# The last block's x in weight buffers, attention placed by time, and the ring's space given up a block sooner

## Chip, core and metric

One NeuronCore of one Trainium2 chip runs the kernel. TensorE (PE) does the matrix products, VectorE (DVE), ScalarE (ACT) and GpSimd (POOL) the elementwise work, and SyncE (SP) issues nearly all DMAs, in the order in which they stand in its queue. The metric is the device time of one execution in microseconds (us), as the median of several runs.

## What is computed

```python
# attention, float32, q, k, v: 4 x 8 heads x 768 x 64; chunks of 32 queries
for c in range(nc):
    k_ctx = k[:, :, l_start:r_end]           # 16 keys left, 8 right of the chunk
    k_full = np.concatenate([mem_k, k_ctx], axis=2)   # v_full likewise
    scores = scale * np.matmul(q_c, k_full.transpose(0, 1, 3, 2))
    scores = scores - np.max(scores, axis=-1, keepdims=True)
    a = np.exp(scores)
    a = a / (np.sum(a, axis=-1, keepdims=True) + 1e-09)
    out[:, :, c_start:c_end] = np.matmul(a, v_full)
# x: 3072 tokens x 512; two layers in a row, 512 -> 2048 -> 512
h = x @ w_in;  g = h - np.tanh(h);  x = g @ w_out
h = x @ w_in2; g = np.maximum(h, 0) + alpha * np.minimum(h, 0); out = g @ w_out2
```

## The kernel before

Every float32 operand of a product is split into a high and a low part (`hi`, `lo`), and three products stand for one (hi·hi, hi·lo, lo·hi).

**Attention** goes by 24 tiles of 128 tokens (t = 0 to 23). For one tile: scores on PE (`sp`, L654), maximum and subtraction on DVE (`mx`, L678; `sc`, L680), exponential on ACT (L722), sum and reciprocal on DVE (`sg`, L733 to L735), the scaling on POOL (`sc`, L740), a transpose on DVE (`et`, L748), copies into `ebuf` on ACT (L761) and POOL (L759), and the values on PE (`pv`, L779). ACT (L788) and DVE (L791) then write the tile's x, in a high and a low part, into the **ring**: two tiles with 8 slots of 128 tokens, in SBUF space of its own.

**Layer 1** goes by 6 blocks of 4 tiles (b = 0 to 5; `blocks1`, N1 = 6). Within a block a loop runs over 16 slices f of the hidden dimension: `h` (L300) is 12 products over x from the ring, then g is made (tanh on ACT, subtraction on DVE, `gh` on ACT L321, `gl` on POOL L322), then `y` (L355) is 12 products. In blocks 4 and 5 only `h` runs, and g is kept (`ga`, `gb`, L336 and L337): their second product is made with layer 2's scheme, one level of a seven-product algorithm, whose products `yb` (L552) follow block 5. Each f has two positions, so that a block is 32 positions; position 0 is the first of block 0.

**Where attention stands.** Blocks use ring slots 0 to 3 and 4 to 7 in turn. `release` in the planning code says from which position a tile may be written: when the block that used its slots has ended. Tiles 20 to 23 (block 5) use the slots of block 3 and may start only at position 127, the end of block 3. The plan keeps steps at least `SPACE` = 6 positions apart, whatever a position lasts (in blocks 4 and 5 it lasts half as long), and step t holds the values of tile t-1 and the scores of tile t. By these rules steps 18 to 24 stand at positions 101, 107, 113, 127, 133, 142 and 148. Loads of a tile's k and q stand LP = 3 positions ahead of its step, the softmax 2 behind it.

**Parking.** Layer 2's weights arrive as float64 (`pk`, L100). They are converted on ACT (`u`, L110) and DVE (L117, L120, L124), combined on DVE (`sm`, L159 to L204), split on ACT and POOL (L133, L134) and written back to DRAM (L152, L149, L170, L175). `PARKS` spreads 88 such steps over the blocks: 1, 23, 18, 26, 8 and 12.

**Buffers.** A pool `w` of 35 tiles of 4 KB a partition holds layer 1's weights (32 tiles until they are used up) and nearly everything else that passes through. After block 5 the ring is closed (`xstack.close()`), and a pool `zr` takes its space, for the tiles `wo` (output weights, 4 buffers, L400) and `t3`. The first four `wo` and block 4 and 5's `t3` are in `w`.

**Layer 2** then has three passes of 8 pairs: `h` (L447) over `wi`, and `yb` over `wo`. `load_in` (L409) loads `wi` two pairs ahead, `load_out` (L400) loads `wo`. Results leave through `st` (L589, L606). The order on each engine outside the first block is made by the compiler's list scheduler from the order in which the code is written.

Of the kernel before, what the change touches and what calls it, by code (L numbers as in the profile page):

```python
# [20 lines left out]
LP, SLACK, LAST_C = 3, 2, 5  # L21
SPACE = 6
# [5 lines left out]
PARKS = ((1, 30, 31), (23, 0, 31), (18, 0, 28), (26, 1, 32), (8, 0, 32), (12, 0, 24))  # L28
BLOCKS2 = [4] * 6
XF = 4  # L30
AHEAD = 5
PAD = 0x1e0
# [4 lines left out]
def chunk_attention_two_ffn_kernel(  # L37
# [24 lines left out]
    blocks2 = BLOCKS2  # L62
    assert sum(blocks1) == NTILE and sum(blocks2) == NTILE
# [215 lines left out]
    slots = slots_of(blocks1 + blocks2)  # L279
    x0 = (slots[:len(blocks1)], slots[len(blocks1):])  # L280
# [9 lines left out]
    def emit_h(l, b, n, f):  # L290
        wi = wts[f, 0].rearrange("p a (k f) -> p a k f", k=KD)
        s0 = x0[l][b]
# [36 lines left out]
    def keep_g(b, f):  # L329
# [131 lines left out]
    def pair_h(i, ahead=None):  # L461
# [4 lines left out]
        if p % 2 == 0:  # L466
# [3 lines left out]
            if i == P2:  # L470
                stage["zr"].tile([128, PAD // 4], FP32, name="pad", bufs=1)
# [315 lines left out]
    def values_hi(t, slot):  # L787
        last["hi"] = nc.scalar.activation(out=ring[0][:, slot], in_=pvt[t], func=ACTF.Copy).ins  # L788

    def values_lo(t, slot):  # L790
        last["lo"] = nc.vector.tensor_tensor(  # L791
            out=ring[1][:, slot], in0=pvt.pop(t), in1=f32(ring[0][:, slot]), op=ALU.subtract
        ).ins

    def emit_pv(t, slot):
        values_mm(t)
        values_hi(t, slot)
        values_lo(t, slot)
# [11 lines left out]
    start2 = [sum(blocks2[:b]) for b in range(len(blocks2))]  # L810
# [11 lines left out]
    def tok_c(t):  # L822
        b, i = first_of[t]
        if t == NS:
            with tc.issue_after(last["h"]):
                emit_pv(t, x0[0][b] + i)
        else:
            emit_pv(t, x0[0][b] + i)
# [17 lines left out]
    if True:  # L846
# [51 lines left out]
        def hi(t):  # L898
            values_hi(t, x0[0][0] + t)

        def lo(t):
            values_lo(t, x0[0][0] + t)
# [297 lines left out]
```

## Time and profile before

| | |
|---|---|
| median of 3 runs | 1072.28 us (1069.95 to 1075.39) |
| the profiled execution, whole | 1071.91 us |
| its span, first to last instruction | 1070.1 us |
| PE busy | 1039.1 us (97%) |
| DVE, ACT, POOL busy | 749.1, 554.1, 456.3 us |
| DMA moved | 225.55 MB, mean 211 GB/s |
| chain of work that ended last | PE 85%, DVE 4%, ACT 3%, DMA 3%, issue 2%, POOL 2% |
| mean granted TensorE clock | 0.996 of full speed |

PE is busy in all but 31 us of the span, about half of them in the first 30 us. The profile tells of each piece of idle time what ended it (an instruction of another engine, a DMA), and the granted clock of any stretch. Where PE waits, the timeline has the wait in brackets behind the instruction that waited.

### The profile page before, as it was taken

How to read it: one execution, taken by the hardware profiler on the slowest of the kernel's cores; microseconds unless marked ns; L12 is line 12 of the kernel's file. 1: busy time of each engine (PE TensorE's matmuls, PEld its weight loads, DVE VectorE, ACT ScalarE, POOL GpSimd, SP SyncE). 2: the span in 40 equal slices, each digit the busy share in tenths (PEclk: the TensorE clock that was granted, in tenths of full speed). 3: DMA queues.
4: the chain of work that ended last, by engine and by line, in shares of the span. 5: the costliest groups of instructions: out<-in, count | busy, mean ns of one | idle time of the engine just before them, and what ended most of it. 6: DMA issues, size and time to landing. Idle time of an engine off the chain costs nothing.

```text
span 1070.1 us, 17570 instructions
## 1 busy us (share of the span) xinstructions
PE 1039.1 (97%) x6576; PEld 849.3 (79%) x6576; DVE 749.1 (70%) x1044; ACT 554.1 (52%) x909; POOL 456.3 (43%) x379
## 2 busy tenths in 40 slices
PE   4999999999999999989999999999999999999998
PEld 3777788888888788778778888888788888788886
DVE  6899768556655776656888755889655889556882
ACT  5677644444544454443536355844356643466640
POOL 3577667755655566235914222205122224123100
PEclk9999999999999999999999999999999999999999
DMA  9885444365665867535678675289773589762575
GB/s 301 287 299 202 134 143 159 118 187 209 211 204 171 276 231 260 169 129 177 243 288 289 242 265 167 85 267 311 232 246 119 161 259 304 259 207 69 176 210 165
DMA packets 118052, 225.55 MB, mean 211 GB/s; under 512 B 37840, under 2 KB 66512, under 8 KB 117968
## 3 DMA queue, kind: packets, MB, share of 16 engines
q1 hardware_dynamic: 113552, 219.98, 62.0%
q10 hardware_dynamic: 4416, 4.46, 1.4%
q8 instruction: 52, 0.85, 0.3%
q14 instruction: 32, 0.26, 0.1%
HBM read 167.78 MB, written 56.62 MB: 210 GB/s over the span
## 4 chain that ended last, share of the span: by engine, by line
PE 85%; DVE 4%; ACT 3%; DMA 3%; issue 2%; POOL 2%; SPq 0%; ACTq 0%; DVEq 0%; POOLq 0%
PE yb L552 28%; PE h L447 21%; PE h L300 19%; PE y L355 15%; PE pv L779 2%; PE sp L654 1%; DMA pk<-in_moe_w_in_dram 1%; POOL ws L134 1%; ACT ebuf L761 1%; DMA wi<-w2i 1%; DMA wo<-w1o 1%; DMA w2i<-ws 1%; ACT eb L761 0%; DVE u L120 0%; DVE u L117 0%
## 5 line engine op out<-in xcount | busy, mean ns | idle before, releaser
L300 PE MATMUL h<-ring,wt 128*128 128x512 f32 x1152 | 281.9, 397 | 2.5 <-ACT ring L788 1.3
L552 PE MATMUL yb<-goh,wo 128*128 128x512 f32 x896 | 279.2, 390 | 1.3 <-DMA wo<-w1o 1.3
L300 PEld LDWEIGHTS h<-ring,wt 128*128 128x128 f32 x1152 | 218.6, 191 | 51.1 <-ACT wt L133 1.6
L447 PE MATMUL h<-xh,wi 128*128 128x512 f32 x672 | 209.8, 390 | 2.6 <-DMA wi<-w2i 1.7
L552 PEld LDWEIGHTS yb<-goh,wo 128*128 128x128 f32 x896 | 168.2, 188 | 37.6 <-issue 2.0
L552 PE MATMUL yb<-gol,wo 128*128 128x512 f32 x448 | 174.3, 389 | 0.0
L447 PEld LDWEIGHTS h<-xh,wi 128*128 128x128 f32 x672 | 126.1, 188 | 29.9 <-DVE h L464 2.1
L355 PE MATMUL y<-gh,wt 128*128 128x512 f32 x512 | 130.3, 394 | 1.0 <-ACT gh L321 1.0
L500 POOL TENSOR_TENSOR t<-gb,ga 128x512 f32<-128x512 f32 x24 | 33.8, 1409 | 202.2 <-DVE ga L457 202.2
L355 PEld LDWEIGHTS y<-gh,wt 128*128 128x128 f32 x512 | 94.3, 188 | 23.0 <-ACT gh L321 1.4
L322 POOL TENSOR_TENSOR gl<-t,gh 128x512 fp32r<-128x512 f32 x64 | 86.8, 1357 | 58.0 <-ACT gh L321 55.2
L552 PEld LDWEIGHTS yb<-gol,wo 128*128 128x128 f32 x448 | 84.1, 188 | 17.5
L525 DVE TENSOR_TENSOR gol<-ga,goh 128x1024 fp32r<-128x1024 f32 x48 | 70.9, 1501 | 21.2 <-ACT goh L534 20.1
L534 ACT ACTIVATE goh<-ga 128x1024 fp32r<-128x1024 f32 x48 | 49.1, 1052 | 62.7 <-DVE ga L525 43.9
L534 ACT ACTIVATE goh<-gb 128x1024 fp32r<-128x1024 f32 x48 | 49.5, 1054 | 57.7 <-DVE gb L525 49.4
L525 DVE TENSOR_TENSOR gol<-gb,goh 128x1024 fp32r<-128x1024 f32 x48 | 70.2, 1488 | 12.9 <-ACT goh L534 12.7
L134 POOL TENSOR_TENSOR ws<-sm,ws 128x512 fp32r<-128x512 f32 x48 | 67.4, 1410 | 26.2 <-ACT ws L133 25.2
L447 PE MATMUL h<-xl,wi 128*128 128x512 f32 x192 | 74.7, 389 | 0.0
L314 DVE TENSOR_TENSOR t<-h,t 128x512 f32<-128x512 f32 x64 | 43.8, 684 | 37.1 <-ACT t L313 36.6
L355 PE MATMUL y<-gl,wt 128*128 128x512 f32 x256 | 68.8, 390 | 0.2 <-POOL gl L322 0.2
L134 POOL TENSOR_TENSOR x<-x,xh 128x1024 fp32r<-128x1024 f32 x9 | 26.9, 2998 | 97.9 <-ACT xh L133 62.9
L313 ACT ACTIVATE t<-h 128x512 f32<-128x512 f32 x64 | 38.0, 593 | 57.9 <-PE h L300 53.7
(112 smaller groups left out, 1571.9 us busy)
## 6 DMA issues: line engine op xcount, KB each, us to landing
wo<-w2o SPq DMA_DIRECT2D x84, 512.0 KB, 4.6
wi<-w2i SPq DMA_DIRECT2D x72, 512.0 KB, 5.5
wo<-w1o SPq DMA_DIRECT2D x28, 512.0 KB, 4.7
kn<-in_k_dram SPq DMA_DIRECT2D x24, 384.0 KB, 5.6
vn<-in_v_dram SPq DMA_DIRECT2D x24, 384.0 KB, 4.5
ri<-in_moe_w_in_dram SPq DMA_DIRECT2D x16, 512.0 KB, 7.1
ro<-in_moe_w_out_dram SPq DMA_DIRECT2D x16, 512.0 KB, 6.5
w1o<-ws SPq DMA_DIRECT2D x32, 256.0 KB, 2.4
```

The source lines that it names most:

```text
L134: nc.gpsimd.tensor_tensor(out=lo, in0=v, in1=f32(hi), op=ALU.subtract)
L300: last["ffn"] = nc.tensor.matmul(out=h, lhsT=wi[:, a, kk, :], rhs=ring[c][:, s0:s0 + n, kk, :], start=(i == 0), stop=(i == 3 * KD - 1),).ins
L313: nc.scalar.activation(out=t, in_=h, func=ACTF.Tanh)
L314: last["dve"] = nc.vector.tensor_tensor(out=t, in0=h, in1=t, op=ALU.subtract).ins
L322: nc.gpsimd.tensor_tensor(out=gl, in0=t, in1=f32(gh), op=ALU.subtract)
L355: mm = nc.tensor.matmul(out=yp[l, b][j][:, :n * 128], lhsT=wo[:, a, j * 128:(j + 1) * 128], rhs=g[c], start=first, stop=final,)
L447: nc.tensor.matmul(out=h, lhsT=w[:, a, 128 * kt:128 * kt + 128], rhs=x[c][:, kt, :], start=(first and j == 0), stop=(j == 5), skip_group_c ...
L500: nc.gpsimd.tensor_tensor(out=d3, in0=gb[1], in1=ga[1], op=ALU.subtract)
L525: last["prep"] = nc.vector.tensor_tensor(out=out, in0=p, in1=q, op=op).ins
L534: nc.scalar.activation(out=hi, in_=src, func=ACTF.Copy)
L552: last["yy"] = nc.tensor.matmul(out=yd[b, into][i], lhsT=w[:, a, i], rhs=op[c][:, p % 2], start=(m == into and p == 0 and n == 0), stop=(p ...
L779: last["at"] = nc.tensor.matmul(out=pv[D * j:D * j + D, 128 * p + 64 * a:128 * p + 64 * a + 64], lhsT=vt[t][:, a, D * h:D * h + D], rhs=e[ ...
```

## The change

Tiles 20 to 23 write their x not into the ring but into four tiles of the pool `w` (`xw`, one for each part and half of the depth), which block 5's `h` reads. Each of these writes becomes two, one for each half. `release` lets these tiles start at position `base[N1 - 3] + 10` = 106, within block 3. The plan measures distances in time: steps are `PIECES` = 17 us apart, the softmax stands 6 us behind its step and loads 9 us ahead, each divided by what a position is taken to last (3.11 us in blocks 0 to 3, 1.56 us in blocks 4 and 5). Steps 18 to 24 now stand at positions 100, 105, 110, 116, 129, 142 and 155. `PARKS` moves two steps from block 3 to block 4 and ends block 5's twelve at position 20, not 24. The ring is closed at the start of block 5, `zr` takes its space there, and holds the first `wo` and the `t3` of blocks 4 and 5. In layer 2's passes `load_out` stands behind the last `load_in`.

```diff
-LP, SLACK, LAST_C = 3, 2, 5
-SPACE = 6
+SLACK = 2
+PIECES = 17
-PARKS = ((1, 30, 31), (23, 0, 31), (18, 0, 28), (26, 1, 32), (8, 0, 32), (12, 0, 24))
+PARKS = ((1, 30, 31), (23, 0, 31), (18, 0, 28), (24, 1, 32), (10, 0, 32), (12, 0, 20))
...
-                out=h, lhsT=wi[:, a, kk, :], rhs=ring[c][:, s0:s0 + n, kk, :],
+                out=h, lhsT=wi[:, a, kk, :],
+                rhs=xw[c, kk // 2][:, kk % 2] if b == N1 - 1 else ring[c][:, s0:s0 + n, kk, :],
...
-            d = t3[0, pp] = w_p.tile([128, 2, 512], FP32, tag="w", name="t3")
+            d = t3[0, pp] = stage["zr"].tile([128, 2, 512], FP32, tag="t3", name="t3")
...
-        pool, tag = (w_p, "w") if i < 4 or i >= NB * NO - P2 // 2 else (stage["zr"], "wo")
+        pool, tag = (w_p, "w") if i >= NB * NO - P2 // 2 else (stage["zr"], "wo")
...
+    def x_parts(t, c):
+        b, i = first_of[t]
+        if b < N1 - 1:
+            return [(slice(None), ring[c][:, x0[b] + i])]
+        if i == 0:
+            for k in range(2):
+                xw[c, k] = w_p.tile([128, 2, 512], FP32R, tag="w", name="xw")
+        return [(slice(2 * k, 2 * k + 2), xw[c, k][:, :, 128 * i:128 * i + 128]) for k in range(2)]
...
+    def values_hi(t):
+        his[t] = x_parts(t, 0)
+        for k, x in his[t]:
+            last["hi"] = nc.scalar.activation(out=x, in_=pvt[t][:, k], func=ACTF.Copy).ins
...
         def release(t):
             b, i = first_of[t]
+            if b == N1 - 1:
+                return base[N1 - 3] + 10
...
+        def slots_in(us, g):
+            return round(us / dur[min(max(0, int(g)) // (2 * NF), len(dur) - 1)])
...
-            lo = max(pos + SPACE, release(t - 1))
+            lo = max(pos + slots_in(PIECES, pos), release(t - 1))
             pos = max(lo, int(at[t]) - SLACK)
-            if t == NTILE:
-                pos = max(lo, min(pos, at[t - 1] + LAST_C))
...
-                todo.append((a + 2, 10 * t + 3, emit_soft, t))
+                todo.append((a + slots_in(6, a), 10 * t + 3, emit_soft, t))
             if t + 1 < NTILE:
-                todo.append((max(a + 1, nxt - LP), 10 * t + 1, loads_to, t + 1))
+                todo.append((max(a + 1, nxt - slots_in(9, nxt)), 10 * t + 1, loads_to, t + 1))
...
+            if b == N1 - 1 and f == 0:
+                xstack.close()
+                stage["zr"] = ctx.enter_context(tc.tile_pool(name="zr", bufs=4, side="right"))
...
+                if f == 11:
+                    load_out(0)
+                    stage["zr"].tile([128, PAD // 4], FP32, name="pad", bufs=1)
+                    load_out(1)
+                elif f == 12:
+                    load_out(2)
+                    load_out(3)
...
-                if f in (12, 13):
-                    load_out(2 * f - 24)
-                    load_out(2 * f - 23)
...
                 if 0 < p < 5:
-                    load_out(b * NO + p - 1)
+                    with tc.issue_after(last["load"]):
+                        load_out(b * NO + p - 1)
```

**ACT, tile 23's softmax in block 4** (`u`, `pk`: parking; `ga`, `gb`: g of block 4 and 5; `sc`: the exponential). Before:

```order
L110 ACTIVATE u<-pk 128x512
L722 ACTIVATE sc<-sc 128x512
L110 ACTIVATE u<-pk 128x512
L336 ACTIVATE gb_5363<-h 128x512 x2
L133 ACTIVATE pk<-wv 128x512
L110 ACTIVATE u<-pk 128x512
L133 ACTIVATE pk<-wv 128x256
L336 ACTIVATE ga_5454<-h 128x512
L761 ACTIVATE ebuf<-et 32x8x32 x4
L133 ACTIVATE pk<-wv 128x4x2x32
L788 ACTIVATE ring_145<-pv 128x512
```

After:

```order
L798 ACTIVATE xw<-pv 128x2x128 x2
L108 ACTIVATE u<-pk 128x512
L719 ACTIVATE sc<-sc 128x512
L335 ACTIVATE gb_5363<-h 128x512
L108 ACTIVATE u<-pk 128x512
L335 ACTIVATE ga_5273<-h 128x512
L758 ACTIVATE ebuf<-et 32x8x32 x4
L335 ACTIVATE gb_5363<-h 128x512
L131 ACTIVATE ws<-sm 128x512
L131 ACTIVATE pk<-wv 128x512
L131 ACTIVATE pk<-wv 128x256
```

Between the exponential and the copies into `ebuf` stood two `u`, two `pk` and three g; now one `u` and two g, and the x that ACT writes ahead of them is tile 22's, in two instructions.

**SP, the end of block 5** (`wo<-w1o`: the weights that `yb` reads first; `w2o<-ws`: parking's last writes). Before:

```order
L400 DMA wo<-w1o_0_117 128x1024
L400 DMA wo<-w1o_1_118 128x1024
L175 DMA w2o_3_112<-ws 128x2x256
L175 DMA w2o_3_108<-ws 128x2x256
L400 DMA wo<-w1o_2_119 128x1024
L175 DMA w2o_3_116<-ws 128x2x256
L175 DMA w2o_3_100<-ws 128x2x256
L400 DMA wo<-w1o_3_120 128x1024
L400 DMA wo<-w1o_0_133 128x1024
```

After, where the first four stand about a whole pair of parked weights earlier:

```order
L168 DMA w2i_87<-ws 128x1024
L173 DMA w2o_3_92<-pk 128x2x256
L399 DMA wo<-w1o_0_117 128x1024
L399 DMA wo<-w1o_1_118 128x1024
L399 DMA wo<-w1o_2_119 128x1024
L399 DMA wo<-w1o_3_120 128x1024
L98 DMA pk<-in_moe_w_out_dram 128x512
L98 DMA pk<-in_moe_w_in_dram 128x512
```

The four loads no longer stand behind the last writes of parking; the fifth (`w1o_0_133`) still does.

**SP, from `yb` into the last pass of layer 2** (`out_dram<-st`: results; `wi`: the weights of the third pair). Before:

```order
L606 DMA out_dram<-st 32x16x64 x4
L400 DMA wo<-w2o_0_89 128x1024
L400 DMA wo<-w2o_1_90 128x1024
L400 DMA wo<-w2o_2_91 128x1024
L400 DMA wo<-w2o_3_92 128x1024
L606 DMA out_dram<-st 32x16x64 x4
L409 DMA wi_9158<-w2i_83 128x1024
```

After:

```order
L603 DMA out_dram<-st 32x16x64 x8
L408 DMA wi_9170<-w2i_83 128x1024
L408 DMA wi_9172<-w2i_83 128x1024
L408 DMA wi_9174<-w2i_83 128x1024
L408 DMA wi_9176<-w2i_83 128x512
L399 DMA wo<-w2o_0_89 128x1024
```

The four loads of `wo` now follow the loads of `wi`, one behind each pair's. On PE the order of layer 2 is the same in both kernels.

## Rows read from the trace of the kernel before

**Rows 1.** PE's waits, whole run: total us, times, longest us

```profile
PE pv L779 <- ACT ebuf L761: 4.0, 2, 2.9
```

**Rows 2.** PE timeline, blocks 3 and 4: start us, us, what, [wait and its releaser]

```profile
363.21 2.11 PE L355 MATMUL y<-gh,wt 128*128 128x512 f32 x8 [0.98 <-ACT gh L321]
365.53 1.20 PE L355 MATMUL y<-gl,wt 128*128 128x512 f32 x4 [0.21 <-POOL gl L322]
...
368.53 3.03 PE L300 MATMUL h<-ring,wt 128*128 128x512 f32 x12
...
425.27 1.15 PE L779 MATMUL pv<-ebuf,vn 96*64 96x64 f32 x32
426.36 0.86 PE L654 MATMUL sp<-kn,qn 64*32 64x64 f32 x64
...
436.65 0.34 PE L779 MATMUL pv<-ebuf,vn 96*64 96x64 f32 x4 [1.04 <-ACT ebuf L761]
437.99 4.53 PE L300 MATMUL h<-ring,wt 128*128 128x512 f32 x12 [1.01 <-DVE gb L337]
...
461.55 0.86 PE L654 MATMUL sp<-kn,qn 64*32 64x64 f32 x64
...
474.39 1.60 PE L779 MATMUL pv<-ebuf,vn 96*64 96x64 f32 x32 [2.91 <-ACT ebuf L761]
```

**Rows 3.** Busy us by engine, granted clock (PEclk), DMA share; block 4's second wait

```profile
436.00:442.50 6.50, 4.84 (x18) 3.54 (x18) 0.69 (x1) 1.18 (x3) 0.67 (x2) 0.74 0.12 43
```

**Rows 4.** The chain that ended last, after block 4's last values

```profile
475.99 4.30 PE h L300 x12
```

**Rows 5.** ACT timeline: the copies into ebuf of tiles 21 and 23

```profile
434.90 1.70 ACT L761 ACTIVATE ebuf<-et 32x256 f32<-32x256 f32 x4 [1.07 <-DVE et L748]
...
472.65 1.69 ACT L761 ACTIVATE ebuf<-et 32x256 f32<-32x256 f32 x4 [0.32 <-DVE et L748]
```

**Rows 6.** DVE timeline: tile 23's x after its values

```profile
476.66 0.69 DVE L791 TENSOR_TENSOR ring<-pv,ring 128x512 fp32r<-128x512 f32 x1 [1.30 <-ACT ring L788]
```

**Rows 7.** The chain that ended last, block 3, ahead of PE's wait at 363

```profile
343.09 5.50 DMA w2i<-ws
...
348.61 5.69 DMA pk<-in_moe_w_in_dram
...
354.38 0.63 ACT u L110
```

**Rows 8.** The chain and PE timeline: from block 5 into yb

```profile
524.64 4.53 POOL ws L134 x2
...
530.10 6.24 DMA wo<-w1o
...
536.48 0.47 PE L552 MATMUL yb<-goh,wo 128*128 128x512 f32 x1 [1.26 <-DMA wo<-w1o]
```

**Rows 9.** SP, chain, DVE and PE: from yb into layer 2's last pass

```profile
915.77 2.12 SPq L400 DMA_DIRECT2D wo<-w2o  x4
919.51 2.40 SPq L606 DMA_DIRECT2D out_dram<-st  x4
921.96 7.04 DMA wi<-w2i
927.51 0.69 DVE L464 TENSOR_TENSOR gb<-h,hv 128x512 f32<-128x512 f32 x1 [0.73 <-ACT hv L491]
929.14 0.47 PE L447 MATMUL h<-xh,wi 128*128 128x512 f32 x1 [1.74 <-DMA wi<-w2i]
```

**Rows 10.** PE timeline: the same place one pass earlier

```profile
774.69 0.47 PE L447 MATMUL h<-xh,wi 128*128 128x512 f32 x1 [0.89 <-DVE gb L464]
```

**Rows 11.** DMA issues: KB each, median us to landing

```profile
wo<-w1o SPq DMA_DIRECT2D x28, 512.0 KB, 4.7
```

**Rows 12.** DVE timeline: one operation with POOL busy beside it, and with POOL idle

```profile
530.33 10.24 DVE L525 TENSOR_TENSOR gol<-ga,goh 128x1024 fp32r<-128x1024 f32 x4 [1.05 <-issue]
...
907.63 1.21 DVE L525 TENSOR_TENSOR gol<-gb,goh 128x1024 fp32r<-128x1024 f32 x1
```

More of the change, by code (lines that the diff above doesn't have):

```diff
@@ L61, in chunk_attention_two_ffn_kernel @@
     blocks1 = BLOCKS1
-    blocks2 = BLOCKS2
-    assert sum(blocks1) == NTILE and sum(blocks2) == NTILE
+    assert sum(blocks1) == NTILE
     def f32(ap):
@@ L277, in slots_of @@
         return go(0, None)
-    slots = slots_of(blocks1 + blocks2)
-    x0 = (slots[:len(blocks1)], slots[len(blocks1):])
+    x0 = slots_of(blocks1)
+    xw = {}
     PASS = ((0, 0), (0, 1), (1, 0))
@@ L291, in emit_h @@
         wi = wts[f, 0].rearrange("p a (k f) -> p a k f", k=KD)
-        s0 = x0[l][b]
+        s0 = x0[b]
         pool, tag = (ps_y, "y") if b >= N1 - 2 and f % 3 else (ps_h, "h")
@@ L469, in pair_h @@
             t3[b, p // 2] = stage["zr"].tile([128, 2, 512], FP32, tag="t3", name="t3")
-            if i == P2:
-                stage["zr"].tile([128, PAD // 4], FP32, name="pad", bufs=1)
         d3 = t3[b, p // 2][:, p % 2]
@@ L785, in values_mm, with values_lo, emit_pv @@
         pvt[t] = pv.rearrange("k (p n) -> k p n", p=HP)
[L787 to L795, printed above, removed]
+    def x_parts(t, c):
[6 more added lines that the diff above has]
+        return [(slice(2 * k, 2 * k + 2), xw[c, k][:, :, 128 * i:128 * i + 128]) for k in range(2)]
+    his = {}
+    def values_hi(t):
+        his[t] = x_parts(t, 0)
+        for k, x in his[t]:
+            last["hi"] = nc.scalar.activation(out=x, in_=pvt[t][:, k], func=ACTF.Copy).ins
+    def values_lo(t):
+        pv = pvt.pop(t)
+        for (k, x), (_, h) in zip(x_parts(t, 1), his.pop(t)):
+            last["lo"] = nc.vector.tensor_tensor(
+                out=x, in0=pv[:, k], in1=f32(h), op=ALU.subtract
+            ).ins
+    def emit_pv(t):
         values_mm(t)
-        values_hi(t, slot)
-        values_lo(t, slot)
+        values_hi(t)
+        values_lo(t)
     spt, sgt, ett, eb, pvt = {}, {}, {}, {}, {}
@@ L809, in chunk_attention_two_ffn_kernel @@
         t0 += n
-    start2 = [sum(blocks2[:b]) for b in range(len(blocks2))]
     nk = [0]
@@ L822, in tok_c @@
     def tok_c(t):
-        b, i = first_of[t]
         if t == NS:
             with tc.issue_after(last["h"]):
-                emit_pv(t, x0[0][b] + i)
+                emit_pv(t)
         else:
-            emit_pv(t, x0[0][b] + i)
+            emit_pv(t)
         if NS < t + 1 < NTILE:
@@ L898, in hi @@
         def hi(t):
-            values_hi(t, x0[0][0] + t)
+            values_hi(t)
         def lo(t):
-            values_lo(t, x0[0][0] + t)
+            values_lo(t)
         def h_mm(f):
@@ L997, in release @@
             b, i = first_of[t]
+            if b == N1 - 1:
+                return base[N1 - 3] + 10
             prev = max([x for x in range(b) if not (
-                x0[0][x] + blocks1[x] <= x0[0][b] + i or x0[0][x] > x0[0][b] + i)], default=None)
+                x0[x] + blocks1[x] <= x0[b] + i or x0[x] > x0[b] + i)], default=None)
             return 0 if prev is None else base[prev] + 2 * NF - 1
```

3 lines of the change are left out of this document (removed).

## The prediction, made before the changed kernel ran

> **What bounds the kernel now.** First the list of PE's waits, since PE is the bound: its largest item behind the first 30 us is the values waiting for ACT's copies into `ebuf` [rows 1]. Then the PE timeline, to see where each wait stands and what it costs beyond its own length; then the chain of waits and the other engines' timelines at those places, to see who came last. The order of instructions on all engines is unchanged up to about 328 us, the end of block 2, so only waits behind that point are at stake. There are six places, and the rest of PE's time is products that the change neither adds nor removes.
>
> 1. Block 3, 363 us: `y` waits 0.98 us for `gh` and 0.21 us for `gl` [rows 2], 1.19 us in all. The chain shows why: a raw weight of parking could only be asked for when a write had landed (343.09 + 5.50), took 5.69 us itself, and ACT stood at its conversion until 354.38 [rows 7]; g was queued behind.
> 2. Block 4, 436 us: values wait 1.04 us, the next `h` 1.01 us, and then 12 products take 4.53 us where such a piece takes 3.03 us [rows 2]. That is 1.50 us more; the granted clock is 0.74 in this stretch [rows 3], so PE ran at the lower of its two levels (1.2 GHz) for a part of it, after about 2 us of idleness.
> 3. Block 4, 474 us: the last tile's values wait 2.91 us, take 1.60 us where others take 1.15 us [rows 2], and the 12 products behind them 4.30 us [rows 4] against 3.03 us. 2.91 + 0.45 + 1.27 = 4.63 us.
> 4. 536 us: `yb` waits 1.26 us for its fourth `wo`. The load was issued at 530.10, when POOL had ended parking's last subtractions (524.64 + 4.53), and took 6.24 us [rows 8].
> 5. Layer 2's second pass, 774 us: 0.89 us, for a DVE addition [rows 10].
> 6. Its third pass, 929 us: 1.74 us, for `wi`, which took 7.04 us [rows 9].
>
> Sum: 1.19 + 3.55 + 4.63 + 1.26 + 0.89 + 1.74 = 13.26 us. The sums below are made against the profiled execution's 1071.91 us (its span is 1070.1 us, 1.8 us lie around it); the median of the runs is 1072.28 us, 0.4 us above, less than the runs differ.
>
> **Part by part.**
>
> *Attention placed by time.* A tile's chain, from the end of its scores to the end of its `ebuf` copies, takes 434.90 + 1.70 - 427.2 = 9.4 us for tile 21 and 472.65 + 1.69 - 462.4 = 11.9 us for tile 23 [rows 2, 5]. What lies between scores and values on PE is counted in the order of the change, at 3.03/12 = 0.25 us a product, less the overlap at a piece's end, so 0.23. Before, tiles 21, 22 and 23 had 36, 58 and 39 products (8 to 13 us), fewer than a chain for two of them: places 2 and 3. Now tiles 21, 22 and 23 have 144, 84 and 72 (33, 19 and 16.5 us): at least 4 us above the longer chain. So places 2 and 3 lose their waits, and with them their time at the lower clock: -3.55 and -4.63 us. Fewer foreign steps on ACT between exponential and copies shorten the chain besides; I take nothing for it.
>
> The price is block 3. Tiles 17, 18 and 19 had 72 products each and now have 60 (13.8 us); tile 20 had 168 and has 72. 13.8 us is 1.9 us above the longest chain that rows show. What eats it is an ACT queue held by a late raw weight, as at place 1. Bounds: nothing (place 1's wait goes as well), and for one of the three tiles the whole excess if a raw weight's 5.69 us stand in its chain, 5.69 - 1.9 = 3.8 us; hardly for all three, since parking's steps in this block fall from 26 to 24. I take 2.0 us where 1.19 us stand now: +0.8 us, range -1.2 to +3 (3.8 in place of 1.19, rounded up).
>
> DVE and POOL share this load, and they slow each other: four `gol` operations take 10.24 us with POOL busy, 2.56 us each, against 1.21 us for one of the same form with POOL idle [rows 12]. The Trainium skill (SBUF — State Buffer, "SBUF: two separate sides") has it that DVE, with two SBUF inputs, and GpSimd lock a shared pair of ports for a whole instruction, and the other blocks; it speaks against packing more of both into block 3. By that rule, an estimate of mine from [rows 12], each of the three dense tiles could lose one such delay, 1.35 us. It is a rival below.
>
> *x in weight buffers.* Four more instructions on ACT and four on DVE, all of these of half the size; beside the products, in engines that wait for PE here. The one place where they lie on the path is the last tile: block 5's first `h` needs its x. Before, DVE ended that x at 477.35, 1.4 us after the values ended at 475.99 [rows 4, 6], with 24 products to spare; now 12 products (2.7 us) stand between. Two halves instead of one add about 0.3 us (copies of half the width take 0.42 us each [rows 5]): 1.7 of 2.7 us. If one g (0.6 to 0.7 us on either engine, as long as the x write in [rows 6]) stands ahead on both, 0.3 us are late. 0 to 1.4 us, taken 0.4. PE's products cost the same from `xw`, whose rows are contiguous.
>
> *Ring space given up sooner; parking ends four positions sooner.* The first four `wo` are asked for about a pair of parked weights earlier and no longer behind parking's last writes: place 4 goes, -1.26 us. What is late next is the fifth `wo`, which now needs the first one's buffer: free 2.7 us (12 products) after `yb` starts, needed 8.2 us later, against 4.7 us for such a load at the median [rows 11] and 6.24 us at its worst here [rows 8]: hidden, with 2 us left. It also still stands behind parking's last writes; these come sooner than `yb` by the two slices of f by which `PARKS` is shortened (24 products, 5.4 us). If both covers go, the wait is as large as before, 1.26 us. Queued behind an early `wo` on SP are two raw weights: should they wait for the ring's last reader, parking in block 5 starts late, and only ACT and DVE notice, whose g have several banks in hand.
>
> *load_out behind load_in.* At place 6 SP issued 2 MB of `wo` at 915.77, results at 919.51, and `wi` only then, at 921.96 [rows 9]. The issue of `wi` does not move, since it stands behind results that wait for DVE; what goes is the 2 MB ahead of it in the DMA engines. It should land well ahead of 929.00. But the same product also waits for a bank that DVE frees: 927.51 + 0.69 = 928.20 [rows 9], as at place 5, where that wait alone is 0.89 us [rows 10]. PE was ready at 929.14 - 1.74 = 927.40, so 0.9 us stay: -0.84 us (0 if `wi` is as slow as before). Place 5 stays as it is. The `wo` themselves are needed only when the pass's eight pairs are done.
>
> **Sum.** -3.55 - 4.63 - 1.26 - 0.84 + 0.8 + 0.4 = -9.1 us: 1071.9 - 9.1 = **1062.8 us**. With the kind ends, -3.55 - 4.63 - 1.26 - 0.84 - 1.2 = -11.5: 1060.4. With the unkind ends, -3.55 - 4.63 + 0 + 0 + 3 + 1.4 = -3.8: 1068.1.
>
> **Rivals.**
>
> *The waits move with the tiles.* Attention's values still come last, in other places: the chains grow with denser work on ACT and DVE, as tile 23's was already 2.5 us longer than tile 21's. For it: three tiles have under 2 us of excess. Against it: places 2 and 3 had 8 to 13 us. If block 3 takes back the gain of place 3, 4.6 us, and `yb`'s wait stays, the gain is 3.55 + 0.84 = 4.4 less 0.4 us: 1067.9 us, no change that can be told.
>
> *Slower: raw weights hold ACT.* In SP's queue `vn`, `kn` and `qn` of a tile now stand ahead of raw weights that they followed, and each waits for a product of the tile before. Each of tiles 17, 18 and 19 then finds ACT standing at a conversion for a whole landing, 5.69 us [rows 7], of which 1.9 us are covered: 3.8 us each, 11.4 us, and a stretch at the lower clock behind each of them as at place 2 (1.50 us): 15.9 us. With places 2, 3, 4 and 6 gone (10.3 us) the kernel stands at 1077.5 us, slower by 5.6 us. It decides from 3.4 us a dense tile on. Against it: the pool `w` has more tiles free through block 3, one with each f, and the only such wait in 300 us before cost 1.19 us.
>
> *DVE and POOL stand in each other's way in block 3.* Each of the three dense tiles loses 2.56 - 1.21 = 1.35 us [rows 12], 4.05 us where the sum has 2.0: 1064.9 us. For it: more of both engines' work in the same time. Against it: the chains of 9.4 and 11.9 us include what POOL did beside them.
>
> *The change does not do what it says.* The scheduler, not the plan, sets the order; but in the order of the change the values stand where the plan puts them. Left is that tiles 21 to 23 wait for something else, loads of `kn` above all: gain 1.26 + 0.84 = 2.1 us, 1069.8 us.
>
> **How the numbers follow.** About half a per cent, 5.4 us, is what a measurement of this kernel can tell from no change. The forecast (about 1060.4 to 1066.9) has 0.58, engines in each other's way 0.12, both faster; waits that move 0.17 and no effect 0.06, both within half a per cent; slower 0.07, of which 0.05 is beyond half a per cent and the rest within it. So faster 0.70, same 0.25, slower 0.05. The range leaves out the slower case and the last of the no-effect case, and goes 1 us below the kind end for the runs' own spread: 1059.5 to 1069.
>
> **What the profile would show.** Right: no wait of `pv` for `ebuf` in blocks 4 and 5, a granted clock of 1.00 from 420 to 520 us, no wait of `yb` for `wo`, and 0.9 us at the start of layer 2's second and third pass. The step on block 3 is wrong if `y` or `pv` there wait over 3 us together; the step on x if block 5's first `h` waits for DVE. The prediction fails if attention's chains in block 3 come out above 14 us, or if the loads that were moved on SP make a new product wait for a DMA.

## The result, and the profile of the changed kernel

| | before | after |
|---|---|---|
| median | 1070.65 us (1069.95 to 1075.39, 5 runs) | 1059.42 us (1058.60 to 1059.95, 5 runs) |
| ratio, with its 95% interval | | 0.9885 (0.9863 to 0.9907) |
| the profiled execution, whole | 1071.91 us | 1059.44 us |
| its span | 1070.1 us | 1057.6 us |
| mean granted clock | 0.996 | 0.999 |

The kernel is faster by 1.15% (0.9 to 1.4%), 12.5 us between the two profiled executions where the forecast was 9.1. 1059.42 us lies just below the low end of the predicted range, 1059.5. So direction and kind were right and the size was too small; which terms were off is told below.

All waits of PE behind the first 110 us, from the PE timeline of the changed kernel (start us, us, what, [wait and its releaser]):

```profile
472.75 2.57 PE L298 MATMUL h<-xw,wt 128*128 128x512 f32 x10 [0.37 <-ACT xw L798]
535.97 0.47 PE L549 MATMUL yb<-goh,wo 128*128 128x512 f32 x1 [0.35 <-ACT goh L531]
539.72 0.47 PE L549 MATMUL yb<-goh,wo 128*128 128x512 f32 x1 [0.75 <-DMA wo<-w1o]
562.04 0.47 PE L549 MATMUL yb<-goh,wo 128*128 128x512 f32 x1 [0.30 <-DMA wo<-w1o]
730.78 0.50 PE L549 MATMUL yb<-goh,wo 128*128 128x512 f32 x1 [0.50 <-DMA wo<-w2o]
```

They sum to 2.27 us. The six places of the kernel before summed to 10.0 us of waits as such, and 13.3 us with the lower clock. None of the values waits for `ebuf` any more ([rows 1] had 4.0 us), nothing waits in block 3 ([rows 2], 1.19 us), nor at the start of a pass of layer 2 ([rows 9, 10]). The stretch of [rows 3] is now full, at the upper level of the clock (2.4 GHz); columns as there:

```profile
436.00:442.50 6.50, 6.50 (x30) 5.40 (x29) 5.90 (x12) 4.05 (x10) 3.78 (x6) 1.00 0.25 97
```

Where the time went is seen from the moments at which PE goes from one part to the next (`yb` begins, `h` of layer 2 begins, and so on), which the PE timeline gives. Lengths in us, with two experiments (E2, E12 below) beside:

| stretch | before | after | E2 | E12 |
|---|---|---|---|---|
| start to layer 1's first `yb` | 526.53 | 516.41 | 516.80 | 520.03 |
| to layer 2's first `h` | 83.51 | 83.83 | 83.73 | 81.69 |
| first `h` pass | 68.00 | 68.00 | 68.00 | 68.00 |
| `yb` behind it | 85.73 | 86.25 | 86.06 | 86.37 |
| second `h` pass | 68.16 | 66.96 | 68.11 | 66.96 |
| `yb` behind it | 85.45 | 85.46 | 85.45 | 85.45 |
| third `h` pass | 68.97 | 66.98 | 68.46 | 66.98 |
| last `yb` | 79.04 | 79.05 | 79.04 | 79.05 |

Between before and after: -10.12 us up to `yb`, +0.32 in layer 1's `yb`, +0.52 in the next `yb`, -1.20 and -1.99 in the second and third `h` pass: -12.5 us.

### The profile page after: what moved, and what is told of

Its sections match the earlier page's. It is cut to its first block, busy times and chain, and to the rows that moved or that the text cites. A ratio compares the mean times of both kernels' runs of the same rounds, so it can differ in the third digit from the quotient of the medians.

```text
span 1057.6 us, 17570 instructions
## 1 busy us (share of the span) xinstructions
PE 1034.3 (98%) x6576; PEld 847.3 (80%) x6576; DVE 752.3 (71%) x1048; ACT 553.8 (52%) x913; POOL 457.2 (43%) x379
## 4 chain that ended last, share of the span: by engine, by line
PE 86%; DVE 5%; ACT 4%; issue 2%; DMA 2%; POOL 1%; SPq 0%; ACTq 0%; DVEq 0%
PE yb L549 24%; PE h L446 21%; PE h L298 20%; PE y L354 16%; PE pv L776 2%; ACT goh L531 1%; PE sp L651 1%; DMA wo<-w2o 1%; POOL t L340 1%; DVE u L118 1%; DMA wo<-w1o 0%; ACT eb L758 0%; DVE u L115 0%; DMA pk<-in_moe_w_in_dram 0%; DVE ga L522 0%
## 5 line engine op out<-in xcount | busy, mean ns | idle before, releaser
L298 PE MATMUL h<-ring,wt 128*128 128x512 f32 x960 | 234.7, 395 | 1.5 <-ACT ring L798 1.3
L298 PEld LDWEIGHTS h<-ring,wt 128*128 128x128 f32 x960 | 180.9, 190 | 41.9 <-ACT wt L131 1.7
```

Of the source, the lines that this page charges most:

```text
L298: last["ffn"] = nc.tensor.matmul(out=h, lhsT=wi[:, a, kk, :], rhs=xw[c, kk // 2][:, kk % 2] if b == N1 - 1 else ring[c][:, s0:s0 + n, kk, ...
```

## Experiments

The change has four parts that can be switched apart: the plan in time (with its three distances), `PARKS`, x in weight buffers together with the ring's space, and `load_out` behind `load_in`. "Longer" and "shorter" below are by medians unless a trace is named.

### Layer 2: load_out alone, and everything but it (E1, E2)

E1 is the kernel before with this edit, E2 the changed kernel without it.

```diff
                 if 0 < p < 5:
-                    load_out(b * NO + p - 1)
+                    with tc.issue_after(last["load"]):
+                        load_out(b * NO + p - 1)
```

> The kernel before with one edit of the change alone: in layer 2's passes the loads of wo stand behind the loads of wi. The forecast's theory (the first product of a pass also waits for a bank that a DVE addition frees): about 0.9 us of PE's wait stay at the start of the second and at the start of the third pass, the first of them named after DVE and as long as before, the gain is 0.84 us at the third pass alone. Its rival (the late wi is the only cause at both places, and the second pass's wait was put down to the wrong releaser): no wait at either place, 0.89 + 1.74 = 2.6 us gained, less at most 0.5 us that a wo of layer 2 may then come late, as in the changed kernel. Neither touches blocks 3 and 4: their waits of 1.19, 2.05 and 2.91 us stay, and yb's 1.26 us in layer 1. Time: about 1070 by the first, 1068.5 by the second, beside 1071 before.

> The changed kernel with that one edit undone; the order on PE stays as in the changed kernel. If the late wi is the only cause, the waits at the start of layer 2's second and third pass come back, 0.9 and 1.7 us, the 0.50 us that yb waited for a wo in the second pass goes, and the time is about 2.1 us longer than the changed kernel's (1061.5 us). If they were cured by something else in the change, they stay away and the time stays at 1059.4 us.

E1 took 1067.41 us (ratio 0.9955, 0.9942 to 0.9969), E2 1063.2 us, 3.8 us longer than the changed kernel. In E1 both waits at the start of a pass are gone, and a `wo` comes late instead; in E2 both are back. PE timeline of E1:

```profile
858.68 0.47 PE L552 MATMUL yb<-goh,wo 128*128 128x512 f32 x1 [1.37 <-DMA wo<-w2o]
```

PE and DVE timeline of E2, the second pass, and its third:

```profile
765.49 0.47 PE L446 MATMUL h<-xh,wi 128*128 128x512 f32 x1 [0.88 <-DVE gb L463]
...
764.72 0.69 DVE L463 TENSOR_TENSOR gb<-h,hv 128x512 f32<-128x512 f32 x1 [0.73 <-ACT hv L488]
...
919.36 0.47 PE L446 MATMUL h<-xh,wi 128*128 128x512 f32 x1 [1.17 <-DMA wi<-w2i]
```

And the same product and the same addition in the changed kernel, whose order on PE and DVE is that of E2:

```profile
764.11 0.61 PE L446 MATMUL h<-xh,wi 128*128 128x512 f32 x2
...
764.60 0.69 DVE L463 TENSOR_TENSOR gb<-h,hv 128x512 f32<-128x512 f32 x1 [0.73 <-ACT hv L488]
```

In E2 the product that waits begins 0.08 us after the addition's end (764.72 + 0.69 = 765.41), which looks like cause and effect. In the changed kernel the same product is the second of the two at 764.11, so it begins at about 764.34, before the addition has even begun. So it never needed that addition. What it waited for, here and in [rows 10], was `wi`: of E2's order only that of SP's loads differs from the changed kernel's. The rival is right, the forecast's "floor" of 0.9 us at both places does not exist: the passes get 1.20 and 1.99 us shorter, and a `wo` takes 0.5 us of it back (1.37 us in E1). The profiled executions, whole, give 2.4 us for E1 (1071.91 - 1069.54) and 2.7 us for the changed kernel against E2 (1062.14 - 1059.44); the medians say 4.8 and 3.8. That is a matter of which execution was profiled: E1's is the slowest of its nine, E2's the fastest of its four. Why repeats of the kernel before and of E1 differ by 4 us and more among themselves, those of the changed kernel by 1.4 us, is not settled.

### Which part carries the gain of blocks 3 and 4 (E3, E4, E7, E11, E12)

E3 is the kernel before with the plan in time alone (x in the ring). E11 is E3 with the new `PARKS`, E12 is E11 with `load_out` behind `load_in`. E4 is the changed kernel with the old distances, E7 the changed kernel with the old `PARKS`. Of each edit the line that matters, in E3, in E11 and (reversed) in E7, in E4; the distances of the softmax and the loads go with the first and the last:

```diff
-            lo = max(pos + SPACE, release(t - 1))
+            lo = max(pos + slots_in(PIECES, pos), release(t - 1))
...
-PARKS = ((1, 30, 31), (23, 0, 31), (18, 0, 28), (26, 1, 32), (8, 0, 32), (12, 0, 24))
+PARKS = ((1, 30, 31), (23, 0, 31), (18, 0, 28), (24, 1, 32), (10, 0, 32), (12, 0, 20))
...
-            lo = max(pos + slots_in(PIECES, pos), release(t - 1))
+            lo = max(pos + SPACE, release(t - 1))
```

> The kernel before with the plan in time alone: steps 17 us apart, x of tiles 20 to 23 in the ring as before, so that tile 20's still waits for block 3's end; parking and the space of the ring as before. Tiles 21, 22 and 23 then have 48, 69 and 51 products between scores and values. Theory (what counts is the number of products against a chain of 9.4 to 11.9 us): the waits at 436 us stay (1.04 + 1.01 us and the time at the lower clock behind them, 3.55 us in all), the last tile's 2.91 us go, and with them 4.6 us of time; block 3 has tiles of 60 products and shows no wait of values. Rival (the plan alone does it, x in weight buffers only makes room): no waits in block 4 at all, over 8 us gained.

> The changed kernel with the old rules of distance (six positions between steps, loads three and softmax two ahead or behind, whatever a position lasts): x stays in weight buffers, so tiles 20 to 23 may start in block 3. Tiles 20 to 23 have 72, 108, 84 and 60 products between scores and values, against chains of 9.4 to 11.9 us (41 to 52 products). Theory (room is all that is needed, the measure of distance hardly matters): no wait of values for the ebuf copies, time within 1 us of the changed kernel's 1059.4. Rival (spacing in time is needed, since softmax two positions behind lies 3 us behind the scores in block 4 and six positions are 9 us there): waits of values of 1 to 3 us in block 4, 1062 to 1064 us.

> The changed kernel with the kernel before's division of parking: 26 steps in block 3, 8 in block 4, and block 5's twelve ending at position 24. Tests whether block 3 needed the two steps fewer. Theory of the forecast (block 3's price is an ACT queue held by raw weights): waits of y or values of 1 to 4 us in block 3, and yb's first wo 1 to 2 us late at the end of block 5. Rival (block 3 has room, the old wait there was tied to one place in its order): no wait in block 3, only yb's grow by up to 1.3 us.

> The run with the plan in time alone, which stood 6.89 us at yb's start for a gol of DVE, with one more line: parking as the change has it (two steps moved from block 3 to block 4, block 5's twelve ending at position 20). x in the ring, and the first wo in the pool w. Theory (there DVE still had parking's steps ahead of the first gol, so time won in block 4 was lost at yb; four positions are 6.2 us): yb's wait falls below 2 us and the time to 1067 to 1070 us. Rival (block 5's raw weights come too late whatever the plan, since tile 23's chain and x hold the engines): the wait stays over 4 us.

> The kernel before with three parts of the change: the plan in time, the new division of parking, and load_out behind load_in. Left out are x in weight buffers and the ring's space given up sooner: tile 20 may start only when block 3 has ended, and the first wo stand in the pool w behind parking's last writes. Theory (the plan and parking carry the gain in blocks 3 and 4, load_out that in layer 2; x in weight buffers and the ring's space are worth the waits that the run without load_out still had there and the changed kernel has not, 1.12 + 0.79 + 0.95 us less 0.4 us, and nothing at yb): 1064.2 - 2.8 = 1061.4 us, 2 us slower than the changed kernel. Rival (x in weight buffers is what makes block 4 free of waits, and the run without load_out was a lucky one): waits of values in block 4 of 2 us and more with stretches at the lower clock, 1064 us or more.

| kernel | plan in time | new PARKS | x and ring's space | load_out | median, us | ratio to before |
|---|---|---|---|---|---|---|
| E3 | yes | | | | 1075.66 | 1.0038 (1.0021 to 1.0055) |
| E11 | yes | yes | | | 1064.18 | 0.9930 (0.9903 to 0.9958) |
| E12 | yes | yes | | yes | 1059.80 | 0.9892 (0.9870 to 0.9914) |
| E4 | | yes | yes | yes | 1067.25 | 0.9961 (0.9948 to 0.9974) |
| E7 | yes | | yes | yes | 1060.98 | 0.9896 (0.9868 to 0.9923) |
| after | yes | yes | yes | yes | 1059.42 | 0.9885 (0.9863 to 0.9907) |

The title part, x in weight buffers with the ring's space, is not what carries the gain: E12 does without it, and its median is 0.4 us from the changed kernel's, less than the runs differ (its theory had 2 us). The plan in time is worth 7.8 us (E4 against after), yet alone it makes the kernel slower (E3). It needs one of two things beside it, the new `PARKS` (E11: 11.5 us shorter than E3) or x and the ring's space (E7), and the second of the two then adds at most 1.6 us.

E3 shows the mechanism. Block 4 does about as the theory says (the last tile's wait is 0.72 us where 2.91 stood). Block 3, where the theory had no wait, has two (values 0.34 us at 375.52, the next `h` 1.29 us) and the lower clock behind them (12 products in 4.62 us). Even so PE comes to the end of block 5 at 523.21 us (530.10 - 6.89), 3.3 us sooner than in the kernel before (526.53), and then stands. PE timeline, SP's queue, then DVE and POOL beside it:

```profile
530.10 0.77 PE L552 MATMUL yb<-goh,wo 128*128 128x512 f32 x1 [6.89 <-DVE gol L525]
...
524.42 0.87 SPq L175 DMA_DIRECT2D w2o<-ws  x2
525.38 0.46 SPq L400 DMA_DIRECT2D wo<-w1o  x1
...
526.59 2.33 DVE L1083 TENSOR_SCALAR alpha_neg<-alpha_sb 128x16 f32<-128x16 f32 x1
528.84 1.21 DVE L525 TENSOR_TENSOR gol<-ga,goh 128x1024 fp32r<-128x1024 f32 x1
...
526.56 2.33 POOL L342 TENSOR_TENSOR ga<-ga,ga 128x1024 f32<-128x1024 f32 x1
```

The bracket names a `gol`, and the expectation of E11 took it at its word. But this `gol` is DVE's fifth, and `yb` does not need it to begin: in the kernel before, `yb` began at 526.53, ahead of the fifth at 530.33 [rows 12], and so it did in E7, at 519.45 against 522.84. What ended the wait is the first `wo`. It was issued at 525.38, took 4.6 us to land (at about 529.96), and stands on SP behind two of parking's last writes, which left at 524.42, when POOL had made what they write. In the kernel before, two `wo` stood ahead of these writes; the first was issued at 522.62, took 3.8 us and landed 0.14 us before `yb` began. So even there a PE that came sooner would have stood for that load, and in E3 the load is 3.6 us later still: what the plan wins in block 4 is lost here. Behind the 6.89 us PE ran at a granted clock of 0.83 from 520 to 540 us. E7 is the counter-test: with the old `PARKS`, but with the first `wo` ahead of parking's last writes, `yb` does not wait, although these writes leave only at 520.59:

```profile
519.45 0.39 PE L549 MATMUL yb<-goh,wo 128*128 128x512 f32 x1
...
522.84 10.10 DVE L522 TENSOR_TENSOR gol<-ga,goh 128x1024 fp32r<-128x1024 f32 x3
...
520.59 3.12 SPq L173 DMA_DIRECT2D w2o<-ws  x4
```

With the new `PARKS` (E11) parking's last writes leave 11 us sooner than in E3, at 513.47, the first `wo` at 515.74, and only 0.82 us of waiting for it are left. Blocks 3 and 4 gain too: PE is there at 519.19 (520.01 - 0.82), 4.0 us sooner than in E3. Both together made E11 faster than its theory (1064.2 us against 1067 to 1070):

```profile
434.85 3.01 PE L300 MATMUL h<-ring,wt 128*128 128x512 f32 x12 [1.12 <-DVE gb L337]
...
470.33 1.15 PE L779 MATMUL pv<-ebuf,vn 96*64 96x64 f32 x32 [0.79 <-ACT ebuf L761]
...
475.38 25.01 PE L300 MATMUL h<-ring,wt 128*128 128x512 f32 x109 [0.95 <-ACT ring L788]
...
520.01 0.47 PE L552 MATMUL yb<-goh,wo 128*128 128x512 f32 x1 [0.82 <-DMA wo<-w1o]
```

The first three of these waits, 2.9 us together, are in E12 too (E11 has 0.31 us more at 409), and none is followed by the lower clock. Of what x in weight buffers and the early `wo` gain there (`yb` 3.6 us sooner in the table of stretches) 2.1 us are lost again in layer 1's `yb`; the profiled executions of E12 and of the changed kernel are 1.6 us apart, the medians 0.4.

E4 missed both theories: no value waits for `ebuf`, and still 7.8 us are lost. 3.1 us go in blocks 3 and 4, in small waits of `y` and `h` (0.24 to 0.53 us) and the pieces between them, and 5.75 us in `yb`, 0.83 being the clock from 520 to 540 us. PE timeline, then SP's queue, of E4; then SP's queue of the changed kernel:

```profile
524.56 0.51 PE L549 MATMUL yb<-goh,wo 128*128 128x512 f32 x1 [2.16 <-ACT goh L531]
526.34 0.80 PE L549 MATMUL yb<-gol,wo 128*128 128x512 f32 x1 [1.28 <-DVE gol L522]
...
479.36 1.74 SPq L399 DMA_DIRECT2D wo<-w1o  x4
481.15 0.45 SPq L98 DMA_DIRECT2D pk<-in_moe_w_out_dram  x1
```

```profile
473.20 1.91 SPq L399 DMA_DIRECT2D wo<-w1o  x4
475.16 0.56 SPq L98 DMA_DIRECT2D pk<-in_moe_w_out_dram  x1
```

Block 5's first raw weights stand behind the early `wo`. In E4 that `wo` goes out when the last product that reads the ring has ended (at 479.33 us), and the raw weights go out 6.0 us later than in the changed kernel. ACT's conversion of the first of them begins at 489.78 us and not at 482.39, and the `goh` for which `yb` stands at 523.46 and not at 512.32. So the two raw weights that the prediction saw behind the early `wo` and priced at nothing probably do cost something as soon as `wo` itself is late. No run moves them alone, and part of the 11.1 us is something else: the last `sm` of parking, ahead of that `goh`, takes 2.50 us on DVE beside an operation of POOL, 0.85 us in the changed kernel. DVE, POOL and ACT of E4, then DVE of the changed kernel:

```profile
520.34 2.50 DVE L202 TENSOR_TENSOR sm<-wv,sm 128x256 f32<-128x256 f32 x1
519.99 2.57 POOL L341 TENSOR_TENSOR ga<-ga,ga 128x1024 f32<-128x1024 f32 x1
522.93 0.63 ACT L131 ACTIVATE ws<-sm 128x512 fp32r<-128x512 f32 x1 [1.91 <-DVE sm L202]
...
510.90 0.85 DVE L202 TENSOR_TENSOR sm<-wv,sm 128x256 f32<-128x256 f32 x1
```

### How dense block 3 may be (E8)

```diff
-PIECES = 17
+PIECES = 12
```

> The changed kernel with steps 12 us apart instead of 17, nothing else: in block 3 the tiles have about 40 products (9 us) between scores and values, less than the chain of 9.4 to 11.9 us that rows of the kernel before show. Theory (a tile's chain against its products decides, and 60 products were enough by 2 us): each of the dense tiles waits 0.5 to 3 us and stretches at the lower clock follow, 3 to 10 us lost in all. Rival (the chain was long only where it stood behind g and conversions on ACT, and is shorter in block 3): no wait, time within 1 us of 1059.4.

1066.3 us (0.9937 to 0.9971 of before), 6.9 us longer than the changed kernel. The theory is right for the one tile that has 40 products between scores and values, tile 18. Tile 17 has 48, the two behind have 64 and 84, and their values do not wait; the rest of the loss are waits of `y` (0.70 and 0.94 us) and of block 5's first `h` (1.07 us), the lower clock, and 0.6 us in layer 1's `yb`. PE and ACT timeline of E8; the scores behind the one row are the tile's whose copies into `ebuf` and values follow:

```profile
343.31 0.86 PE L651 MATMUL sp<-kn,qn 64*32 64x64 f32 x64
...
354.48 1.69 ACT L758 ACTIVATE ebuf<-et 32x256 f32<-32x256 f32 x4 [1.29 <-DVE et L745]
...
356.23 0.34 PE L776 MATMUL pv<-ebuf,vn 96*64 96x64 f32 x4 [2.53 <-ACT ebuf L758]
357.26 3.58 PE L354 MATMUL y<-gh,wt 128*128 128x512 f32 x8 [0.70 <-ACT gh L320]
```

And one dense tile of the changed kernel:

```profile
360.65 0.86 PE L651 MATMUL sp<-kn,qn 64*32 64x64 f32 x64
...
372.06 1.70 ACT L758 ACTIVATE ebuf<-et 32x256 f32<-32x256 f32 x4 [1.47 <-DVE et L745]
...
375.27 1.15 PE L776 MATMUL pv<-ebuf,vn 96*64 96x64 f32 x32
```

The chain is 12.0 us in E8 (344.17 to 356.17) and 12.25 us in the changed kernel (361.51 to 373.76), a little above the longest that the prediction had (11.9). In the changed kernel the values begin 1.5 us behind these copies (375.27 - 373.76), 1.2 us behind POOL's, which end at 374.11. So 60 products cover the chain, by a margin that is small but whole, and 40 do not. E7 shows how near the edge is. With two more parking steps in block 3, the values of a tile come out in two pieces, the first behind 52 products, waits of 0.33 and 1.28 us appear, and the lower clock behind them (12 products in 4.61 us). E3, which has these steps too, shows the same:

```profile
374.93 0.34 PE L776 MATMUL pv<-ebuf,vn 96*64 96x64 f32 x4 [0.33 <-ACT ebuf L758]
376.55 4.61 PE L298 MATMUL h<-ring,wt 128*128 128x512 f32 x12 [1.28 <-DVE t L313]
```

### The wo of layer 1 (E5, E6, E9, E10)

E5 puts the fifth to eighth `wo` into the pool `w`; E10 moves block 4's and 5's results from SP's queue to ACT's besides. E6 puts the first four `wo` back into `w` as before the change, with the padding of `zr` ahead of the other `wo`; E9 is E6 with the padding behind them, as in the changed kernel.

```diff
-        pool, tag = (w_p, "w") if i >= NB * NO - P2 // 2 else (stage["zr"], "wo")
+        pool, tag = (w_p, "w") if 4 <= i < 8 or i >= NB * NO - P2 // 2 else (stage["zr"], "wo")
...
-            nc.sync.dma_start(out=y1d[N1 - 2 + t, :, 2 * h:2 * h + 2, :], in_=st)
+            nc.scalar.dma_start(out=y1d[N1 - 2 + t, :, 2 * h:2 * h + 2, :], in_=st)
...
-        pool, tag = (w_p, "w") if i >= NB * NO - P2 // 2 else (stage["zr"], "wo")
+        pool, tag = (w_p, "w") if i < 4 or i >= NB * NO - P2 // 2 else (stage["zr"], "wo")
...
-                    stage["zr"].tile([128, PAD // 4], FP32, name="pad", bufs=1)
...
         wo2[i] = w
+        if i == 4:
+            stage["zr"].tile([128, PAD // 4], FP32, name="pad", bufs=1)
```

The first edit is E5, with the second E10; the third is E6, with the last two E9.

> The changed kernel with one line altered: the fifth to eighth wo of layer 1 go to buffers of the pool w and not to those that the first four leave. The order on PE, DVE, ACT and POOL is the same; on SP these four loads now stand up to eight rows sooner, ahead of the loads of x for layer 2. Theory (yb's three waits in the changed kernel, 0.35 + 0.75 + 0.30 us at 536 to 562 us, follow from the fifth wo waiting for a buffer and the ninth standing behind four loads of x): the 0.75 and 0.30 us go, the 0.35 us for ACT stay, about 1.0 us gained: 1058.4 us. Rival (the DMA engines are full there, busy share 0.9, and whatever is moved ahead makes something else late): the sum of yb's waits stays within 0.4 us of 1.4, or returns at layer 2's first products as a wait for x or wi; no gain.

> The run with the fifth to eighth wo in the pool w, with one more line altered: block 4's and 5's results of layer 1 (y1d<-st) are issued by ACT and not by SP. In that run SP stood at the first of them until 557.18 us, and the wo behind it came 1.96 us late at 562. Theory (the wait at 562 is SP's order: a result in front of a load): SP issues that wo some 5 us sooner, no wait of yb for wo at 562, yb's sum of waits under 0.5 us where the changed kernel has 1.40, 1058 us. Rival (DMA bandwidth is the limit there): the wait stays at 1 us or more.

> The changed kernel with the first four wo in the pool w again, as before the change; the ring's space is still given up at the start of block 5 and holds t3 and the later wo. On SP the first four loads then stand behind parking's last writes again. Theory (place 4's wait came from that order in SP's queue): yb waits 1.3 us for its fourth wo as before; the changed kernel's three waits (1.40 us in all) go or stay, and the time is 0 to 1.3 us longer. Rival (parking's earlier end is enough): no wait for the first four wo, and the time is the same or shorter, 1058.5 to 1059.4 us.

> The run with the first four wo in the pool w, with one more line moved: the 480 bytes of padding in the ring's old space are taken behind the four wo buffers, as in the changed kernel, and not ahead of them. The order on every engine is the same as in that run; only the addresses of the wo buffers differ. In that run three products of yb took 0.70 us where they take 0.68 us in the changed kernel, at a granted clock of 1.00, all through layer 2, and it lost 7 us there. Theory (the address of wo does it): 0.68 us again, stretches of yb of 85.4 us and not 87.7, and only what the late first wo cost stays: a wait of about 2.3 us at yb's start with some of the lower clock behind it, 1061 to 1063 us. Rival (a wo buffer in the pool w is read slower): 0.70 us stay, at least while the first four are used, and the time stays near 1069.

E5 took 1059.99 us and E10 1058.86 us (0.9863 to 0.9910 and 0.9850 to 0.9880 of before): neither can be told from the changed kernel. In E5 the waits at 536 and 540 us go, that for ACT too, and 1.96 us appear at 562. In E10 that one goes, and 1.26 and 0.69 us appear at 577 and 585. PE timeline and SP's queue of E5, then of E10:

```profile
562.55 0.47 PE L549 MATMUL yb<-goh,wo 128*128 128x512 f32 x1 [1.96 <-DMA wo<-w1o]
...
557.18 0.32 SPq L586 DMA_DIRECT2D y1d<-st  x1
557.59 3.35 SPq L399 DMA_DIRECT2D wo<-w1o  x4
```

```profile
576.56 0.50 PE L549 MATMUL yb<-goh,wo 128*128 128x512 f32 x1 [1.26 <-DMA wo<-w1o]
...
563.65 7.85 SPq L408 DMA_DIRECT2D wi<-w2i  x2
571.59 0.38 SPq L399 DMA_DIRECT2D wo<-w1o  x1
```

Each time the wait of `yb` stands behind the next row of SP's queue that itself waits: a result not yet written, then two `wi` whose buffers are not free. Moving a load past one of them finds the next, and the sum of `yb`'s waits (1.40 us in the changed kernel) stays at 1.96 and 1.95 us. E10's theory is right about the wait at 562, but neither run came to the time that its theory had (1058.4 and 1058 us).

E6 took 1068.95 us, 9.5 us longer than the changed kernel, which neither theory had. E9, with the same order on every engine, took 1060.91 us. The products of `yb` over a whole run (us in all, mean ns of one), of the changed kernel, E6 and E9:

```profile
L549 PE MATMUL yb<-goh,wo 128*128 128x512 f32 x896 | 279.4, 389 | 1.9 <-DMA wo<-w1o 1.0 <-DMA wo<-w2o 0.5 <-ACT goh L531 0.4
```

```profile
L549 PE MATMUL yb<-goh,wo 128*128 128x512 f32 x896 | 285.1, 396 | 2.3 <-DMA wo<-w1o 2.3
```

```profile
L551 PE MATMUL yb<-goh,wo 128*128 128x512 f32 x896 | 280.3, 391 | 2.3 <-DMA wo<-w1o 2.3
```

What cost 8 us of the 9.5 was the address. With the four `wo` buffers 480 bytes further on, three products of `yb` take 0.70 us and not 0.68, at a granted clock of 1.00, and each stretch of `yb` in layer 2 is 1.5 to 2.3 us longer. The rest, 1.5 us by the medians, is what it costs to have the first four `wo` behind parking's last writes: E9 waits 2.31 us for the first `wo` at 518.75, and nowhere else in `yb`.

## Why the prediction fell short, step by step

| step | forecast | measured | |
|---|---|---|---|
| places 2 and 3 | -8.18 | -9.5 | waits gone as forecast, 1.3 us more came back |
| block 3 | +0.8 | -1.19 | no wait is left at all |
| block 5's first `h` waits for x | +0.4 | +0.37 | as forecast |
| place 4 | -1.26 | +0.32 | the waits move on |
| place 5 | 0 | -1.20 | wrong releaser |
| place 6 | -0.84 | -1.99 | no floor |
| a `wo` of layer 2 | 0 | +0.52 | not foreseen |
| sum | -9.1 | -12.7 | |

The measured column comes from the stretches and the waits. The first row is what is left of the stretch from 328 us to `yb`, which is 10.36 us shorter, after the two rows below it (-10.36 + 1.19 - 0.37 = -9.5). The sum is 0.2 us off because block 3 begins 0.24 us later in the changed kernel's profile.

**The two steps that failed, 2.0 and 2.35 us.** The first is block 3's price. The prediction computed an excess of 1.9 us over the longest chain and then charged 2.0 us all the same, for a raw weight that might stand in it. Measured are 1.5 us of excess at tile 19, more at tiles 17 and 18, and no wait; its own lower bound, -1.2, was the right value. There is luck in it: the longest chain that the prediction used, 11.9 us, is of block 4, and in block 3 of the kernel before tile 18's took 13.6 us (348.36 to 361.98), nearly all of the 13.8 us that 60 products give. In the changed kernel it takes 8.9 us. PE and ACT timeline of the kernel before:

```profile
347.50 0.86 PE L654 MATMUL sp<-kn,qn 64*32 64x64 f32 x64
...
360.28 1.70 ACT L761 ACTIVATE ebuf<-et 32x256 f32<-32x256 f32 x4 [1.15 <-DVE et L748]
```

The second failed step is the floor in layer 2. It rested on one releaser, a DVE addition in [rows 10], and on an addition that ended at 928.20 in [rows 9]; E2 and the changed kernel show that PE does not need it.

**Place 4** was a wrong step in the other direction, 1.6 us. The first four `wo` are in time. The ninth, issued at 530.21 us behind four loads of x, is not: it took 9.4 us to land where the fifth took 3.6. Nor is one at 562. For 562 and later, E5 and E10 show SP's order; whether at 540 it is the order or the full DMA engines (a share of 0.94 from 530 to 540 us) was not separated.

**Places 2 and 3** went as forecast. Of the 1.3 us more, 0.6 us are time behind the waits that the prediction did not count: 216 products from 475.92 us to 526.53 take 50.61 us where 216 x 0.2267 = 48.97 us would do, 1.64 us and not 1.27, and the 12 products of [rows 2] at 437.99 lost 1.74 us and not 1.50 up to the next one's start. Not all of that is the lower clock: 0.15 us of the first is `yb`'s first product, which waited for its `wo`, and the same 12 products lose 0.23 us in E1 at a granted clock of 1.00. The other 0.7 us are left over by subtraction and were not shown.

**The rivals.** Waits moved with the tiles into block 3 only in E8, E7 and E3, not in the changed kernel, and the change did what it says. The slower case, raw weights that hold up their readers, did not happen in block 3; E4 points to it in block 5, and E3 shows another slower case that the prediction had not thought of, PE at the end of block 5 too soon for its first `wo`. That DVE and POOL stand in each other's way is real but left no wait in block 3: an operation on DVE that takes 0.16 us in the changed kernel took 2.33 us in E3, as long as POOL's beside it and ending with it, and `yb` stood there for its `wo`, not for the `gol` behind it. In front of something that PE waited for, such a pair stands at the end of parking in E4 (2.50 us where the changed kernel has 0.85). The Trainium skill (SBUF — State Buffer, "SBUF: two separate sides") describes a lock on a shared pair of ports for a whole instruction, for DVE with two SBUF inputs, as that `sm` has, or in a mode of two ports; the trace agrees. Among the operations that can take such a mode the same page of the Trainium skill has `tensor_scalar`, which is the operation of E3; in which mode it ran no run shows.

## What to carry to other kernels

Where a plan removes waits, look at what stands at the next meeting point: the plan in time was worth 7.5 us together with the new `PARKS` (E11) and less than nothing alone (E3), where the first load that PE needed next stood behind parking's last writes. A releaser in a profile is a coincidence of times until a run moves one of the two; before a floor or a theory is built on it, look for a second thing that landed at that moment: here it was a load both times, in [rows 10] and at the 6.89 us of E3. Switch the parts of a change apart: here its title part was worth nothing that could be measured once the plan's distances and `PARKS` were right.

## What the runs showed of the hardware

**A wait of one length costs the lower clock in one execution and not in another.** E1 has the two waits of [rows 2] at place 2 again, 1.04 and 1.01 us, with the same work around them. There the 12 products took 4.53 us, here 3.02 us, and the granted clock of this stretch is 1.00 where [rows 3] have 0.74:

```profile
437.63 0.34 PE L779 MATMUL pv<-ebuf,vn 96*64 96x64 f32 x4 [1.04 <-ACT ebuf L761]
438.98 3.02 PE L300 MATMUL h<-ring,wt 128*128 128x512 f32 x12 [1.01 <-DVE gb L337]
...
437.00:443.50 6.50, 4.85 (x105) 3.87 (x108) 1.38 (x2) 2.25 (x5) 0.68 (x2) 1.00 0.10 37
```

E3 has the same waits (1.05 and 1.01 us) and again 3.02 us at 1.00. In E7 1.6 us of waits were enough for the lower clock. So the 1.50 us that the prediction charged to place 2 are those of one execution.

**The address of the buffers of `wo` in SBUF changed the rate of the products by 3%** (0.70 against 0.68 us for three) through 480 bytes of padding, with clock and order unchanged (E6, E9). Which property of the address does it was not tried.
